# Transposes of P moved into the score slot for 27 early chunks, swapped q of four pairs by DMA, and a new instruction order

## The chip, the cores and the metric

The kernel runs on one core of one Trainium2 chip. The metric is the device time of one execution in microseconds (us); before the change it is 802.02 us, the median of three runs (799.81 to 802.18). The engines of the core are TensorE (PE in the profile; its weight loads are the row PEld), VectorE (DVE), ScalarE (ACT), GpSimd (POOL) and SyncE (SP), which issues all DMAs here.

## The reference, cut to what matters

```python
q_pool = q.reshape(B, H, S // 2, 2, D).mean(axis=3)      # B, H, S, D = 4, 8, 1152, 64
scores = np.matmul(q_pool, k.transpose(0, 1, 3, 2)) / np.sqrt(D)
attn = softmax(scores)                                    # over the 1152 keys
x = np.matmul(attn, v)  ->  2304 tokens x 512
r = np.maximum(x @ w_in, 0.0)                             # 512 x 2048
out = (r * r) @ w_out                                     # 2048 x 512
```

Everything is float32. The kernel multiplies most of it as pairs of float16 numbers, high part and low part, and some of it directly in float32.

## The kernel before, in words

The attention is cut into 16 pairs of heads (`prep(n)`, n = 0 to 15), and each pair into nine chunks of 128 query rows, 144 chunks in all (`chunk(i)`). A feed-forward block (`block(j)`) takes 256 tokens as soon as the four pairs of a batch that hold them are done, so after a first stage attention and feed-forward alternate on PE.

**Pairs.** `prep` loads k, q and v (LK, LQ, LV), scales them, splits them into high and low float16 parts and transposes them by DMA into `kT` (KT, line 628) and `qT` (QT, line 641). The scores also need a copy of `qT` with its two 64-partition halves swapped. That is QX, line 650: two copies of 64 x 1152 float16 per pair, each on DVE or on POOL. The code has a third branch, two DMAs issued by SP, for the pairs listed in `QXD`; before the change the list is empty. Pair 0 is handled in float32 and has no QX.

**Chunks.** S (`scores`, lines 750 and 755) writes 128 x 1152 scores into one of two score slots in PSUM, `sts[i % 2]`, of three banks with 512 columns each; the third bank holds only 128 columns of scores. MX (DVE, line 766) scales them and finds the row maximum; EX (ACT, line 790) writes P = exp(...) to SBUF and so frees the slot for chunk i + 2. For pairs 0 to 3 (chunks 0 to 35, the early chunks) P stays float32 and is transposed on PE: nine 128 x 128 transposes in three groups (TP, `tp4`, line 831), each group into one of the two banks `ba` of resource "a", from which TC (`tc4`: ACT at line 841 or DVE at line 843) copies it to `PT`. The banks "a" also serve the products P x v (PV, lines 942 and 950), the feed-forward products and many small products; from the end of the attention on, six more banks `bt` serve the feed-forward part. From chunk 36 on P is split into two float16 parts and transposed by DMA (HI and LO, lines 794 to 802, and TR, line 805).

**Weights.** During the early chunks the two weight matrices are loaded, normalised and split (`weights`, lines 1217 to 1341), on ACT, DVE and POOL.

**Order.** `Plan.order` makes the program order of every engine ahead of time. Each step has a cost per engine, dependencies, a due time (its chunk number, plus an offset per kind of step from `CFG['off']` and, for early ones, `CFG['off0']`) and perhaps a choice of engines; the planner simulates the five engines and picks the step with the smallest due time among those that can start soon (`sl...` says how soon; `pen` and `bl` weigh the choice of engine). Steps with `take` hold a bank or a buffer until a step with `give` returns it. Each engine then runs its list strictly in that order, with semaphores between engines. SP's list holds all loads, transposes and stores, so whatever stands behind a waiting DMA on SP waits too.

```python
for x in range(3):
    add(("TP", i, x), {"PE": 400}, [("EX", i)] + ring + ([("TP", i, x - 1)] if x else []), lambda o, x=x: tp4(o, x), i, take=(("TP", i, x), ("a",), 0), give=("P", i) if x == 2 else None)
    add(("TC", i, x), alt("TC", ACT=380, DVE=460), [("TP", i, x)] + ring, lambda o, x=x: tc4(o, x), i, give=("TP", i, x))
```

Of the kernel before, what the change touches and what calls it, by code (L numbers as in the profile page):

```python
# [22 lines left out]
def cfg(k, d):  # L23
    return CFG.get(k, d)


COST = {
# [6 lines left out]
}  # L34


class Clock:


    W = 3413.3  # L40
# [188 lines left out]
def kernel(  # L229
# [182 lines left out]
    def ringof(vi, j):  # L412
# [5 lines left out]
        for v_, r_ in reversed(pairs_[: pairs_.index((vi, r))]):  # L418
            if left and not other and (visits[v_][0] in full_v) != (n in full_v):
                left, other = set(range(0, 896, 64)), True  # L420
            w = 320 if r_ else 256
            hit = left & {c for h in base(v_, r_) for c in range(h, h + w, 64)}
            if hit:
                out.append(("PV", v_, r_))
                left -= hit
        return out

    def prep(n):
        pair = preps[n]["pair"]
# [3 lines left out]
        old = [("S", both(preps[p0]["last"])[0])] if p0 is not None else []  # L433
# [27 lines left out]
        if n == 0 and n in full_s:  # L461
            sk = k[b, 2 * hp : 2 * hp + 2].rearrange("h (p c) d -> p h (c d)", c=9)
            tk = rk

            def lk(o, x):
                nc.sync.dma_start(out=tk().rearrange("p h c d -> p h (c d)")[:, :, 192 * x : 192 * x + 192], in_=sk[:, :, 192 * x : 192 * x + 192])

            for x in range(3):
                add(("LK", n) + ((x,) if x < 2 else ()), {"SP": 900}, [], lambda o, x=x: lk(o, x), need, take=None if x else (("k", n), ("raw",), 0), after=[("LK", n, x - 1)] if x else prev)
        else:  # L470
            add(("LK", n), {"SP": 2500}, [], lambda o: load_kv(rk(), k), need, take=(("k", n), ("raw",), 0), after=prev)
        add(("LQ", n), {"SP": 2600}, [], load_q, need, take=(("q", n), ("raw",), 0), after=[("LK", n)])
        if n in full_v:
            add(("LF", n), {"SP": 2200}, oldv, lambda o: load_kv(v4(slot), v), visits[vs[0]][2], after=[("LQ", n)])
        else:
            add(("LV", n), {"SP": 2200}, [], lambda o: load_kv(rv(), v), need, take=(("v", n), ("raw",), 0), after=[("LQ", n)])

        def qsum(o):
# [227 lines left out]
    def chunk(i):  # L706
# [16 lines left out]
        def scores4(o):  # L723
            kt, qt = k4(n), q4(qT(n))
            for x in range(3):
                k0, k1 = 4 * x, min(4 * x + 4, 9)
                w = 128 * (k1 - k0)
                for y in both(i):
# [3 lines left out]
                    else:  # L732
# [720 lines left out]
```

## Time and profile before

| what | us |
|---|---|
| median of three runs | 802.02 |
| the profiled execution | 804.16 |
| its span, first to last instruction | 802.3 |
| PE busy in it | 742.4 |
| DVE busy | 582.9 |
| ACT busy | 575.4 |
| POOL busy | 383.0 |

The profiled execution has a span of 802.3 us, and 1.86 us lie around it. The mean granted clock of PE is 0.977 of full speed. In the profile, "busy" is the time in which an engine has an instruction running; a row of the timeline or of the waits ends with the idle time of the engine ahead of an instruction and with what ended that idle time.

### The profile page before, as it was taken

How to read it: one execution, taken by the hardware profiler on the slowest of the kernel's cores; microseconds unless marked ns; L12 is line 12 of the kernel's file. 1: busy time of each engine (PE TensorE's matmuls, PEld its weight loads, DVE VectorE, ACT ScalarE, POOL GpSimd, SP SyncE). 2: the span in 40 equal slices, each digit the busy share in tenths (PEclk: the TensorE clock that was granted, in tenths of full speed). 3: DMA queues.
4: the chain of work that ended last, by engine and by line, in shares of the span. 5: the costliest groups of instructions: out<-in, count | busy, mean ns of one | idle time of the engine just before them, and what ended most of it. 6: DMA issues, size and time to landing. Idle time of an engine off the chain costs nothing.

```text
span 802.3 us, 15287 instructions
## 1 busy us (share of the span) xinstructions
PE 742.4 (93%) x5998; PEld 491.7 (61%) x5998; DVE 582.9 (73%) x897; ACT 575.4 (72%) x894; POOL 383.0 (48%) x255
## 2 busy tenths in 40 slices
PE   4969788887899999998899999999999999999997
PEld 3546555544675577546666676577567657785654
DVE  3888999858799896888988899877888864202211
ACT  5776888778797888777897888788888854503412
POOL 2453633258676476365585656585666331001300
PEclk8888999999799999999999999999999999999999
DMA  8587383304999999999799999999999992000011
GB/s 285 207 218 214 119 239 136 75 9 90 219 187 202 192 227 210 211 209 183 159 212 210 207 207 208 211 201 213 204 209 199 182 189 46 1 1 14 14 27 27
DMA packets 324199, 127.77 MB, mean 159 GB/s; under 512 B 306976, under 2 KB 307744, under 8 KB 324128
## 3 DMA queue, kind: packets, MB, share of 16 engines
q1 hardware_dynamic: 324128, 126.80, 76.6%
q8 instruction: 47, 0.77, 0.4%
q14 instruction: 24, 0.20, 0.1%
HBM read 45.09 MB, written 4.72 MB: 62 GB/s over the span
## 4 chain that ended last, share of the span: by engine, by line
PE 42%; DVE 6%; DMA 4%; ACT 3%; issue 3%; POOL 1%; SPq 0%; ACTq 0%; DVEq 0%
PE ba L1163 9%; PE ba L1114 9%; PE bt L1163 6%; PE bt L1114 6%; PE s L755 5%; PE ba L950 5%; DVE s L766 2%; DMA PT<-buf 2%; DMA raw<-in_v_dram 1%; DVE region L1141 1%; ACT buf L794 1%; DMA kT<-buf 1%; PE s L750 1%; ACT buf L790 1%; DVE buf L802 1%
## 5 line engine op out<-in xcount | busy, mean ns | idle before, releaser
L766 DVE TENSOR_SCALAR_CACHE_REDUCE s<-s,esc 128x1152 f32<-128x1152 f32 x135 | 190.3, 1419 | 23.0 <-PE s L755 21.0
L1114 PEld LDWEIGHTS <-w 128*128 128x128 f16 x1728 | 169.1, 99 | 28.8 <-issue 3.2
L802 POOL TENSOR_TENSOR buf<-buf,buf 128x1152 f16<-128x1152 f32 x63 | 159.6, 2535 | 53.6 <-ACT buf L794 40.0
L790 ACT ACTIVATE buf<-s,ca 128x1152 f32<-128x1152 f32 x144 | 174.5, 1213 | 9.6 <-POOL ca L776 3.9
L755 PE MATMUL s<-kT,qT 128*128 128x512 f16 x720 | 136.6, 328 | 9.2 <-ACT buf L790 8.7
L1163 PE MATMUL ba<-w,region 128*128 128x512 f16 x624 | 142.3, 379 | 0.0
L1163 PEld LDWEIGHTS <-region 128*128 128x128 f16 x864 | 82.4, 98 | 95.6 <-issue 1.9
L1114 PE MATMUL ba<-region,w 128*128 128x256 f16 x1128 | 131.5, 274 | 1.2 <-DVE region L1041 0.5
L755 PEld LDWEIGHTS <-qT 128*128 128x128 f16 x720 | 64.0, 100 | 65.0 <-issue 16.5
L1141 POOL TENSOR_TENSOR region<-region 128x512 f16<-128x512 f32 x32 | 42.2, 1320 | 102.1 <-ACT region L1134 101.5
L950 PE MATMUL ba<-PT,v 128*64 128x320 f16 (+1 forms) x1296 | 84.7, 287 | 2.2 <-DMA PT<-buf 2.1
L794 ACT ACTIVATE buf<-buf 128x1152 f16<-128x1152 f32 x71 | 82.4, 1160 | 6.0 <-DMA PT<-buf 2.3
L950 PEld LDWEIGHTS <-v 128*64 128x64 f16 x1296 | 71.1, 110 | 15.0 <-issue 6.2
L802 DVE TENSOR_TENSOR buf<-buf,buf 128x1152 f16<-128x1152 f32 x45 | 67.5, 1501 | 16.2 <-ACT buf L794 11.6
L831 PE MATMUL ba<-ident,buf 128*128 128x128 f32 x324 | 51.6, 289 | 15.5 <-DVE PT L843 8.3
L1129 ACT ACTIVATE region<-region 128x512 f16<-128x512 f32 x72 | 45.0, 626 | 27.7 <-PE bt L1163 19.1
L1141 DVE TENSOR_TENSOR region<-region 128x512 f16<-128x512 f32 x40 | 39.1, 980 | 30.7 <-ACT region L1134 30.3
L831 PEld LDWEIGHTS ba<-ident,buf 128*128 128x128 f32 x324 | 35.2, 144 | 30.4 <-DVE PT L843 9.9
L1163 PE MATMUL bt<-w,region 128*128 128x512 f16 x240 | 52.6, 379 | 0.0
L1124 ACT ACTIVATE region<-ba 128x512 f32<-128x512 f32 x39 | 23.0, 591 | 36.8 <-PE ba L1114 36.8
L841 ACT ACTIVATE PT<-ba 128x384 f32<-128x384 f32 x74 | 34.0, 490 | 20.7 <-PE ba L831 20.0
L1114 PE MATMUL bt<-region,w 128*128 128x256 f16 x408 | 45.9, 273 | 0.0
(180 smaller groups left out, 993.9 us busy)
## 6 DMA issues: line engine op xcount, KB each, us to landing
raw<-in_q_dram SPq DMA_DIRECT2D x32, 288.0 KB, 3.7
raw<-in_k_dram SPq DMA_DIRECT2D x15, 576.0 KB, 4.6
region<-in_moe_w_in_dram SPq DMA_DIRECT2D x8, 1024.0 KB, 6.6
region<-in_moe_w_out_dram SPq DMA_DIRECT2D x8, 1024.0 KB, 5.3
raw<-in_v_dram SPq DMA_DIRECT2D x12, 576.0 KB, 4.7
out_dram<-half SPq DMA_DIRECT2D x20, 128.0 KB, 2.5
v<-in_v_dram SPq DMA_DIRECT2D x4, 576.0 KB, 7.1
out_dram<-buf SPq DMA_DIRECT2D x16, 128.0 KB, 2.4
```

Of the source, the lines that this page charges most:

```text
L755: nc.tensor.matmul(s[:, x, :w], lhsT=qt[:, l].rearrange("p c m -> p (c m)")[:, 128 * c0 + h : 128 * c0 + h + 255 : 2], rhs=rhs, **st)
L766: nc.vector.tensor_scalar(st3(), st3(), sc, 3e38, op0=ALU.mult, op1=ALU.min, accum_out=a[:, x : x + 1])
L790: nc.scalar.activation(P(), st3(), AF.Exp, bias=a[:, 1:2], scale=s1, accum_out=col)
L794: nc.scalar.activation(hl()[:, 0], P(), AF.Copy)
L802: e.tensor_tensor(out=hl()[:, 1], in0=P(), in1=hl()[:, 0], op=ALU.subtract)
L831: nc.tensor.matmul(t[:, y], lhsT=P()[:, c * 128 : (c + 1) * 128], rhs=ident, is_transpose=True, start=(y == 0), stop=(y == 2), skip_group_ ...
L841: nc.scalar.activation(out, t, AF.Copy)
L950: nc.tensor.matmul(px[h * 64 : (h + 1) * 64, 64 * r * (1 - h) : 64 * r * (1 - h) + N], lhsT=vv[:, h, kc, vl, :], rhs=p2(vi, r, h, 9 * pl + ...
L1114: nc.tensor.matmul(ph[:, f2], lhsT=w16[0][:, SLOT[f // 4], wl, a, f % 4 * 128 : (f % 4 + 1) * 128], rhs=xhl()[:, xl, a], start=(i == 0), s ...
L1129: nc.scalar.activation(gt[u][:, 0], rt[u % 2], AF.Square)
L1141: e.tensor_tensor(out=gt[u][:, 1], in0=rt[u % 2], in1=gt[u][:, 0], op=ALU.subtract)
L1163: nc.tensor.matmul(p[:, :DM], lhsT=g[:, gl, f % 2, tt * 128 : (tt + 1) * 128], rhs=w16[1][:, SLOT[f // 4], wl, f % 4], start=(f == 0 and g ...
```

## The change

1. `HYB` lists chunks 9 to 35, the early chunks of pairs 1, 2 and 3. For these the first of the three transpose groups (columns 0 to 383 of P) is written to columns 128 to 511 of the third bank of the chunk's own score slot. It takes no bank of resource "a" and gives none back. The other two groups stay as they were.
2. The score step of a chunk whose slot was so used two chunks earlier (chunks 11 to 37) is split: S does the first two banks, and a new step SB does the third. SB waits for S and for the eviction TC(i - 2, 0) of the transposes in that bank. MX now waits for SB. The number of matmuls and weight loads is the same.
3. `QXD` is (1, 2, 3, 4): for these pairs the two copies of QX become two DMAs from SBUF to SBUF, issued by SP behind the landing of QT.
4. All offsets, slacks and weights of the planner have new values, and some planned costs do too (`LK`, `LQ`, `KT`, `QT`, `TR`, `ST`, `LO` on POOL, the first weight load). So the order changes in the whole kernel, and with it the choice of engine of those steps that have one.

```diff
-CFG = {..., 'slPE': 10.8333, 'slACT': 264.0828, 'slDVE': 159.9116, 'off': {...}, 'off0': {...}, ...}
+CFG = {..., 'slPE': 143.7987, 'slACT': 193.3687, 'slDVE': 104.16, 'off': {...}, 'off0': {...}, ..., 'QXD': (1, 2, 3, 4), ..., 'HYB': (9, 10, ..., 35)}
...
-        def scores(o):
+        def scores(o, xs=(0, 1, 2)):
...
-                for x in range(3):
+                for x in xs:
...
-            add(("S", i), {"PE": 1115 if CH[j] is None else 985}, [("KT", n), ("QX", n, 0), ("QX", n, 1)] + back, scores, i, give=("kT", n) if end else None)
+            two = i - 2 in hyb
+            sd = [("KT", n), ("QX", n, 0), ("QX", n, 1)]
+            if two:
+                add(("S", i), {"PE": 985 if CH[j] is None else 870}, sd + back, lambda o: scores(o, (0, 1)), i)
+                add(("SB", i), {"PE": 150 if CH[j] is None else 130}, sd + back + [("S", i), ("TC", i - 2, 0)], lambda o: scores(o, (2,)), i, give=("kT", n) if end else None)
+            else:
+                add(("S", i), {"PE": 1115 if CH[j] is None else 985}, sd + back, scores, i, give=("kT", n) if end else None)
...
+            def st3_():
+                return sts[i % 2][:, 2, 128:].rearrange("p (a b) -> p a b", b=128)
+
             def tp4(o, x):
-                t = bank(o, 3, 128)
+                t = st3_() if i in hyb and not x else bank(o, 3, 128)
...
+    hyb = {i for i in cfg("HYB", ()) if chunks[i][0] in full_v and chunks[i][0] not in full_s}
```

## Rows read from the trace of the kernel before

**Rows 1.** The page's first part: busy time, share and instructions of each engine.

```profile
PE 742.4 (93%) x5998; PEld 491.7 (61%) x5998; DVE 582.9 (73%) x897; ACT 575.4 (72%) x894; POOL 383.0 (48%) x255
```

**Rows 2.** Busy time by stretch; last columns: granted clock, DMA share, GB/s.

```profile
0.00:60.00 60.00, 41.40 (x308) 28.78 (x309) 39.41 (x61) 39.96 (x61) 26.66 (x22) 0.88 0.76 236
60.00:160.00 100.00, 86.57 (x689) 56.98 (x691) 92.81 (x151) 80.36 (x125) 38.46 (x26) 0.97 0.54 158
160.00:206.00 46.00, 34.30 (x240) 19.21 (x236) 33.12 (x60) 36.80 (x49) 32.41 (x15) 0.89 0.33 71
206.00:640.00 434.00, 422.42 (x3592) 283.95 (x3594) 371.70 (x540) 359.21 (x571) 265.80 (x176) 0.99 1.08 202
640.00:802.00 162.00, 157.70 (x1179) 102.83 (x1173) 45.89 (x87) 59.11 (x92) 19.71 (x17) 1.00 0.21 41
```

**Rows 3.** Groups of instructions, 60 to 160 us: count, busy, mean ns, idle before.

```profile
L766 DVE TENSOR_SCALAR_CACHE_REDUCE s<-s,esc 128x1152 f32<-128x1152 f32 x26 | 36.5, 1419 | 2.9 <-PE s L755 2.5 <-PE s L750 0.3
L790 ACT ACTIVATE buf<-s,ca 128x1152 f32<-128x1152 f32 x25 | 30.4, 1225 | 2.9 <-DVE s L766 2.9
...
L841 ACT ACTIVATE PT<-ba 128x384 f32<-128x384 f32 x44 | 20.2, 490 | 11.9 <-PE ba L831 11.5
...
L843 DVE COPY PT<-ba 128x384 f32<-128x384 f32 x19 | 10.0, 550 | 0.8 <-PE ba L831 0.8
```

**Rows 4.** Waits, 0 to 206 us: who for whom, total us, times, longest.

```profile
ACT PT L841 <- PE ba L831: 20.0, 23, 3.1
...
PE ba L831 <- DVE PT L843: 8.3, 10, 3.0
...
DVE s L766 <- PE s L755: 6.3, 6, 3.3
...
PE ba L831 <- ACT PT L841: 4.8, 15, 0.9
```

**Rows 5.** Timeline of PE, 103 to 112 us: start, us, instruction, idle before.

```profile
103.78 0.93 PE L831 MATMUL ba<-ident,buf 128*128 128x128 f32 x6 [0.25 <-ACT PT L841]
105.36 1.14 PE L755 MATMUL s<-kT,qT 128*128 128x512 f16 x6 [0.65 <-ACT buf L790]
...
111.02 0.55 PE L831 MATMUL ba<-ident,buf 128*128 128x128 f32 x3 [0.72 <-DVE PT L843]
```

**Rows 6.** Line 650 (QX), 0 to 206 us: ns minimum/median/maximum, first and last start.

```profile
L650 POOL COPY qT<-qT x5: 1139/1140/1143, 43.3 to 151.1; 64x1152 f16<-64x1152 f16 x5
...
L650 DVE COPY qT<-qT x3: 475/627/1335, 44.3 to 104.4; 64x1152 f16<-64x1152 f16 x3
```

**Rows 7.** Timelines of POOL and of DVE at 72 us.

```profile
72.31 1.14 POOL L650 COPY qT<-qT 64x1152 f16<-64x1152 f16 x1 [2.25 <-DMA qT<-half]
...
72.43 1.33 DVE L650 COPY qT<-qT 64x1152 f16<-64x1152 f16 x1
```

**Rows 8.** DMA issues by line, whole run: KB each, median us to landing.

```profile
raw<-in_k_dram SPq DMA_DIRECT2D x3, 192.0 KB, 2.6
...
qT<-half SPq DMA_TRANSPOSE x13, 3.3
```

**Rows 9.** Timelines of SP and of PE, 39 to 46 us.

```profile
39.39 1.45 SPq L641 DMA_TRANSPOSE qT<-buf  x1
40.94 0.53 SPq L450 DMA_DIRECT2D raw<-in_k_dram  x1
...
45.26 1.06 PE L547 MATMUL ba<-raw 128*128 128x128 bf16 x9 [1.66 <-DMA raw<-in_k_dram]
```

**Rows 10.** Timelines of DVE and of PE ahead of the first block's products.

```profile
188.73 0.15 DVE L1071 TENSOR_SCALAR xs<-xs 128x1 f32<-128x1 f32 x1
...
198.30 0.15 DVE L1082 RECIPROCAL xs<-xs 128x1 f32<-128x1 f32 x1
...
206.11 0.59 PE L586 MATMUL ba<-acc,cols 128*128 128x1 f32 x2 [2.22 <-ACT v L573]
206.56 4.05 PE L1114 MATMUL ba<-buf,w 128*128 128x256 f16 x24
```

More of the change, by code (lines that the diff above doesn't have):

```diff
@@ L432, in prep @@
         p0 = preps[n]["old"]
-        old = [("S", both(preps[p0]["last"])[0])] if p0 is not None else []
+        old = [("SB" if preps[p0]["last"] - 2 in hyb else "S", both(preps[p0]["last"])[0])] if p0 is not None else []
         keep = preps[n]["slot"] is None
@@ L470, in prep @@
         else:
-            add(("LK", n), {"SP": 2500}, [], lambda o: load_kv(rk(), k), need, take=(("k", n), ("raw",), 0), after=prev)
-        add(("LQ", n), {"SP": 2600}, [], load_q, need, take=(("q", n), ("raw",), 0), after=[("LK", n)])
+            add(("LK", n), {"SP": 2350}, [], lambda o: load_kv(rk(), k), need, take=(("k", n), ("raw",), 0), after=prev)
+        add(("LQ", n), {"SP": 2450}, [], load_q, need, take=(("q", n), ("raw",), 0), after=[("LK", n)])
         if n in full_v:
-            add(("LF", n), {"SP": 2200}, oldv, lambda o: load_kv(v4(slot), v), visits[vs[0]][2], after=[("LQ", n)])
+            add(("LF", n), {"SP": 2250}, oldv, lambda o: load_kv(v4(slot), v), visits[vs[0]][2], after=[("LQ", n)])
         else:
-            add(("LV", n), {"SP": 2200}, [], lambda o: load_kv(rv(), v), need, take=(("v", n), ("raw",), 0), after=[("LQ", n)])
+            add(("LV", n), {"SP": 2250}, [], lambda o: load_kv(rv(), v), need, take=(("v", n), ("raw",), 0), after=[("LQ", n)])
         def qsum(o):
@@ L814, in chunk @@
         else:
-            add(("S", i), {"PE": 1115 if CH[j] is None else 985}, [("KT", n), ("QX", n, 0), ("QX", n, 1)] + back, scores, i, give=("kT", n) if end else None)
+            two = i - 2 in hyb
[5 more added lines that the diff above has]
+                add(("S", i), {"PE": 1115 if CH[j] is None else 985}, sd + back, scores, i, give=("kT", n) if end else None)
         fused = n in scaled_
         ge_ = [] if n in full_s else [("GE", n, "qk")]
-        add(("MX", i), {"DVE": 1340 if fused else 1275}, [("S", both(i)[0])] + (ge_ if fused else []), smax, i, give=("qT", n) if end else None)
+        add(("MX", i), {"DVE": 1340 if fused else 1275}, [("SB", i) if i - 2 in hyb and n not in full_s else ("S", both(i)[0])] + (ge_ if fused else []), smax, i, give=("qT", n) if end else None)
         if fused and n not in full_v:
@@ L845, in chunk @@
             for x in range(3):
-                add(("TP", i, x), {"PE": 400}, [("EX", i)] + ring + ([("TP", i, x - 1)] if x else []), lambda o, x=x: tp4(o, x), i, take=(("TP", i, x), ("a",), 0), give=("P", i) if x == 2 else None)
-                add(("TC", i, x), alt("TC", ACT=380, DVE=460), [("TP", i, x)] + ring, lambda o, x=x: tc4(o, x), i, give=("TP", i, x))
+                add(("TP", i, x), {"PE": 400}, [("EX", i)] + ring + ([("TP", i, x - 1)] if x else []), lambda o, x=x: tp4(o, x), i, take=None if i in hyb and not x else (("TP", i, x), ("a",), 0), give=("P", i) if x == 2 else None)
+                add(("TC", i, x), alt("TC", ACT=380, DVE=460), [("TP", i, x)] + ring, lambda o, x=x: tc4(o, x), i, give=None if i in hyb and not x else ("TP", i, x))
             return
@@ L1268, in weights @@
                     ring = [r for r in ring if r in plan.at]
-                    add((W + "L", c), {"SP": 3050}, ring, wl, at)
+                    add((W + "L", c), {"SP": 5000 if c == 0 else 3050}, ring, wl, at)
                     wx = [("WD", 0, 3)] if w == 1 and i == 3 else []
```

10 lines of the change are left out of this document (5 added, 5 removed), and 2 rows, old and new, of the table COST.

## The prediction

> **What bounds the kernel now.** I read the page's busy shares first. PE is busy for 93% of the span, so at most 60 us can be won by filling its gaps [rows 1]. The second view, busy time by stretch, says where they are [rows 2]: 18.6 us idle in the first 60 us, 13.4 from 60 to 160, 11.7 from 160 to 206, and only 11.6 in the 434 us from 206 to 640 and 4.3 in the tail. From 206 us on, PE is the bound. What the change does by name lies ahead of that point, and a microsecond won there comes off the end, since the rest follows at PE's pace.
>
> From 60 to 160 us the tightest engine is DVE, with 92.8 of 100 us busy; ACT has 80.4 and POOL 38.5 [rows 2]. The third view, groups of instructions of that stretch, shows what DVE does: 26 MX of 1.42 us each (36.5 us) and 19 evictions of transposes of 0.55 us (10.0 us), beside splitting weights, k and q [rows 3]. ACT carries 44 evictions of 0.49 us there. The fourth view, the waits up to 206 us, shows what two banks do to a chunk with three transpose groups: PE stands 8.3 us for evictions by DVE and 4.8 us for evictions by ACT, 13.1 in all, and ACT stands 20.0 us because no transposes have come [rows 4]. The timeline shows single cases: the last groups of a chunk start 0.25 us after an eviction by ACT, or 0.72 us late behind one by DVE [rows 5]. So the stretch is bound by DVE, and ACT loses time to a ring of two banks.
>
> **The change part by part.** The sum is made against the profiled execution, 804.16 us (span 802.3 and 1.86 around it). That is 2.1 us above the median shown, so I take 2.1 off at the end. About 0.3% (2.4 us) is what a measurement of this kernel can tell from no change.
>
> *Swapped q, on DVE and POOL.* Eight copies leave the engines, all ahead of 206 us: three on DVE, 0.475, 0.627 and 1.335 us, 2.4 together, and five on POOL of 1.14 us [rows 6]. POOL has slack, so its 5.7 us count for nothing by themselves. Two of the three DVE copies fall in the stretch where DVE is the bound, 2.0 us. I take 1.5 off, between 0 (if DVE's list just gains a gap) and 2.4. The long DVE copy ran beside a POOL copy that began 0.12 us earlier and held on until 73.45 [rows 7]; alone, a copy takes 0.475. The Trainium skill (SBUF — State Buffer, "Who interferes with whom") has a rule for this: DVE and GpSimd share one pair of ports as an exclusive lock, and the later one blocks. By it each of the five POOL copies could have held DVE up for its full 1.14 us, and the sum would be 4.2 us lower; the row shows 0.86 us of delay once.
>
> *Swapped q, on SP.* Eight DMAs of 64 x 1152 x 2 bytes, 147 KB, are added. The nearest row is a load of 192 KB, 2.6 us from issue to landing, and 0.53 us is what issuing a k load took [rows 8, 9]. So qT is complete some 3 us later than with copies. The scores wait for k's transpose too, so that much may be covered. What can show is SP's order: QX waits for QT's landing, 3.3 us [rows 8], and what stands behind it on SP waits too. After the QT of pair 1 comes the k load of pair 2, for which PE already stood 1.66 us [rows 9]. If SP blocked there the loss is up to 3.3 us; four such places are at most 13 us, were all uncovered, but later loads have raw buffers to wait for anyway, and the planner can put other issues into the gap. I take +0.5, range 0 to 3.3.
>
> *First transpose group in the score slot.* The work is the same: same transposes, same evictions. What goes is the claim of 27 of 108 groups on the two banks; with two groups left per chunk, all nine transposes of a chunk can be issued in a row. If the waits of those 27 of 36 chunks go, PE gets back 0.75 x 13.1 = 9.8 us and ACT 0.75 x 20.0 = 15 us [rows 4]. That is not yet time, because DVE is the bound. It becomes time as ACT takes evictions from DVE: evened out, DVE and ACT would each have (92.8 + 80.4) / 2 = 86.6 us, 6.2 less for DVE, some 11 of its 19 evictions moved [rows 2, 3]. I take 5 off; bounds 0 (no eviction moves) and 10 (PE's whole 9.8).
>
> *The split score step.* The third bank of the next score in this slot waits for an eviction; MX and PE's next instructions stand behind it. Before: EX ends, six matmuls of 1.14 us, MX [rows 5]. After: EX ends, three transposes (0.55), 0.25 of waiting, the eviction (0.49), 0.25 again, two narrow matmuls (by columns 256/2304 of 1.14, 0.13), MX: 1.67 us, 0.53 more, while the wide ones run in that time [rows 3, 5]. Does a slot have that time? 26 MX in 100 us is 3.85 us a chunk, 7.7 a slot [rows 3], and the loop MX, EX, score needs some 4.5 us with its waits; 0.5 more fits. But chunks come in bursts. I take +1.5, between 0 and 27 x 0.53 = 14.
>
> *The new order.* It can't be worked out by hand; I bound it by idle time that it could fill or open. One visible case: the step at 198.30 needs only the one at 188.73, but stands behind other work on DVE, and the first products of the feed-forward part start at 206.56, behind a gap of 2.22 us on PE [rows 10], one of several that make 11.7 us from 160 to 206 [rows 2]. An order that runs this step at once wins up to 9.6 us, less than that idle time; a bad order costs as much there, or doubles the 11.6 us of idle PE in the long stage [rows 2]. I take 2 off, the size of the one gap shown; range -9.6 to +11.6.
>
> Sum: -1.5 + 0.5 - 5 + 1.5 - 2 = -6.5. 804.16 - 6.5 - 2.1 = **795.5 us**.
>
> **The rivals.**
> (a) *DVE keeps the bound.* The bank waits vanish but ACT's and PE's time is only idled elsewhere, no eviction changes engine, and the order gives nothing. For it: DVE stood just 6.3 us for scores [rows 4], so it was fed. Against: ACT has 20 us free in the same stretch and can take evictions. Also here: the change does not do what it says, because the two groups left still meet other users of the two banks. Only the 1.5 us of DVE copies remain, given back by SP and SB: 802.0, within 0.3%.
> (b) *The score waits for the eviction* (slower). The eviction in the third bank stands behind a 1.2 us EX or MX in its engine's list, PE stands at SB, and DVE, already the bound, waits for its scores. It decides as soon as MX's wait for scores grows by more than the 6.5 us that I count on. Price: 14 us if all 27 pay their 0.53; with -5 for the banks, -1.5 and +0.5 for q and nothing for the order that makes 802.0 + 8 = 810.0. The Trainium skill (PSUM — Partial Sum Buffer, "PSUM bank collisions raise a hardware error") speaks against the change here: two engines must be kept apart by bank, not by address, so free columns of a bank in use aren't free. That is why the wait exists; no run here shows a collision. Against (b): the 7.7 us per slot above.
> (c) *The order costs in the long stage* (slower). From 206 to 640 DMA is fully used (share 1.08), with PE idle for only 11.6 us [rows 2]; a later start of a few transposes shows at once. With that idle time doubled and the early gain of 4.5 kept (-6.5 without the order's -2): 802.0 - 4.5 + 11.6 = 809.1.
> (d) *The order fills the gaps ahead of 206 us too*: three quarters of the 9.6, -7.2 in place of -2, and the full 10 for the banks: 802.0 - 10 - 7.2 - 1.5 + 0.5 + 1.5 = 785.3. For it: the late step of [rows 10]. Against: it needs two things at once.
>
> **How the numbers follow.** Forecast 0.48 (own range 788 to 799), (d) 0.12, (a) 0.18, (b) 0.11, (c) 0.11. Faster by over 0.3% (below 799.6): 0.48 + 0.12 = 0.60. Within: 0.18. Slower (above 804.4): 0.22. The range reaches to (d), 785, and up to 808, which takes in (a) and the cheaper half of (b) and (c).
>
> **What would show it.** Right: the wait of ACT for transposes falls from 20.0 to under 10 us, evictions on DVE from 60 to 160 us from 19 to about 10, the first feed-forward product comes at about 200 us instead of 206.6, and the time from there to the end stays near 596 us. Line 650 has no copies ahead of 200 us on DVE and POOL. Wrong: DVE's wait for scores up to 206 us grows past 13 us (b); PE's idle time behind the first feed-forward product grows past 20 us (c); the first product comes no earlier (a).

## The result: slower by 0.9%, and the profile after

The changed kernel takes 810.25 us (median; 805.5 to 813.83) against 802.48 us for the kernel before, timed beside it (799.77 to 806.99): a ratio of 1.0091, 95% interval 1.0066 to 1.0116. Slower, and above the range that was given. The profiled execution took 812.57 us, with a span of 810.8 and a mean granted clock of 0.970 (before 802.3 and 0.977). A trace shows one execution; those read below took between 6 us less (e18) and 5 us more (e15) than the median of their kernel's runs.

The page's first part after the change (before: [rows 1]):

```profile
PE 747.4 (92%) x5998; PEld 492.1 (61%) x5998; DVE 598.6 (74%) x957; ACT 589.3 (73%) x874; POOL 311.9 (38%) x207
```

PE has the same 5998 matmuls and is busy 5.0 us longer; DVE and ACT have 15.7 and 13.9 us more to do, POOL 71.1 us less. So, beside the eight copies of q, the new order moved work from POOL to DVE and ACT.

Busy time by stretch after the change (columns as in [rows 2], which answer to the first four and the last row), with the long stage cut into pieces:

```profile
0.00:60.00 60.00, 43.89 (x337) 29.60 (x337) 39.82 (x68) 36.85 (x57) 24.35 (x22) 0.91 0.79 256
60.00:160.00 100.00, 82.72 (x663) 55.70 (x662) 87.26 (x129) 80.29 (x131) 46.64 (x27) 0.95 0.56 151
160.00:206.00 46.00, 41.16 (x301) 26.95 (x300) 36.20 (x63) 37.38 (x49) 26.07 (x15) 0.95 0.27 63
206.00:640.00 434.00, 415.46 (x3480) 273.66 (x3479) 382.14 (x601) 368.36 (x538) 197.50 (x133) 0.98 1.08 203
...
640.00:811.00 171.00, 164.14 (x1223) 106.16 (x1220) 53.23 (x99) 66.46 (x102) 17.31 (x13) 0.99 0.22 44
...
206.00:280.00 74.00, 71.39 (x587) 47.20 (x585) 67.88 (x108) 65.99 (x95) 26.52 (x19) 1.00 1.12 203
280.00:330.00 50.00, 47.48 (x365) 29.84 (x366) 39.55 (x60) 39.46 (x57) 16.43 (x14) 1.00 1.10 209
330.00:380.00 50.00, 39.80 (x334) 24.83 (x334) 41.91 (x84) 37.30 (x55) 19.42 (x11) 0.80 1.01 194
380.00:460.00 80.00, 78.19 (x663) 51.57 (x660) 72.83 (x106) 67.06 (x101) 44.01 (x29) 1.00 1.11 203
460.00:640.00 180.00, 178.60 (x1539) 120.22 (x1538) 159.97 (x249) 158.55 (x233) 91.12 (x62) 1.00 1.07 203
```

The same pieces of the long stage before:

```profile
206.00:280.00 74.00, 72.51 (x592) 48.20 (x594) 63.54 (x87) 62.16 (x98) 45.28 (x30) 0.98 1.06 197
280.00:330.00 50.00, 50.00 (x444) 35.66 (x441) 41.42 (x63) 43.90 (x74) 33.38 (x23) 1.00 1.13 216
330.00:380.00 50.00, 45.74 (x386) 29.22 (x385) 41.90 (x72) 37.34 (x57) 25.25 (x19) 0.97 1.09 202
380.00:460.00 80.00, 76.00 (x636) 50.51 (x635) 71.98 (x97) 66.15 (x109) 51.68 (x29) 1.00 1.01 195
460.00:640.00 180.00, 178.17 (x1544) 120.35 (x1544) 152.86 (x225) 149.67 (x238) 110.20 (x78) 1.00 1.10 204
```

Busy time times granted clock is a rough measure of the matmul work that PE got through. Summed up to 206 us it is 41.40 x 0.88 + 86.57 x 0.97 + 34.30 x 0.89 = 150.9 before [rows 2] and 43.89 x 0.91 + 82.72 x 0.95 + 41.16 x 0.95 = 157.6 after: PE is **6.7 us ahead** (the other traces with these two early orders give 152.0 to 155.8, in e5, e6, e9 and e17, and 158.9 and 161.2, in e10 and e18). It keeps that lead to 280 us (+7.0). Then 280 to 330 costs 2.5, and 330 to 380 costs 12.5 (44.4 before, 31.8 after: 10.2 us idle, and the rest at a clock of 0.80). From there on PE is **some 8 us behind**, wins 2.6 back by 640 us, loses some 3 in the tail (6.9 us idle there in place of 4.3) and ends 8.5 us later. So the lead is lost on one stretch of 100 us in the middle of the stage in which I had taken PE for the bound.

What the lead is made of shows in two counts. Up to 206 us the changed kernel has done 96 feed-forward matmuls (12.6 us on PE, of which some 11.1 would be left at the full clock, at which 24 take 2.78), the kernel before none:

```profile
L1123 PE MATMUL ba<-buf,w x96: 272/273/421, 174.9 to 204.6; 128*128 128x256 f16 x96
```

So apart from feed-forward work PE is some 4 us behind. From 60 to 160 us, where the change by name was made, it got through 5.4 us less (78.6 against 84.0). The row maxima, one for each chunk, are behind too. Those of pairs 1 and up, from 0 to 206 us, before and after (beside nine of pair 0 in either):

```profile
L766 DVE TENSOR_SCALAR_CACHE_REDUCE s<-s,esc x33: 1405/1418/1427, 62.7 to 204.2; 128x1152 f32<-128x1152 f32 x33
...
L766 DVE TENSOR_SCALAR_CACHE_REDUCE s<-s,esc x31: 1406/1422/1427, 57.6 to 202.3; 128x1152 f32<-128x1152 f32 x31
```

At 160 us it is 31 chunks in place of 35, at 206 us 40 in place of 42 (40 to 42 and 42 to 44 in the traces with the same early orders). From 206 to 640 us both kernels take 98 chunks, 4.4 us each, so two chunks are worth 8.9 us, near the 8.5 by which the changed kernel ends later. That the two chunks are the loss is a reading of these traces; no run moves them alone.

What the change did where it was made, first the evictions of transposes from 60 to 160 us (columns as in [rows 3]):

```profile
L850 ACT ACTIVATE PT<-ba 128x384 f32<-128x384 f32 x38 | 17.5, 491 | 6.3 <-PE ba L840 5.9
L850 ACT ACTIVATE PT<-s 128x384 f32<-128x384 f32 x16 | 7.8, 494 | 3.0 <-PE s L840 1.8 <-PE s L755 1.0
L852 DVE COPY PT<-ba 128x384 f32<-128x384 f32 x8 | 4.3, 550 | 0.4 <-PE ba L840 0.3
...
L852 DVE COPY PT<-s 128x384 f32<-128x384 f32 x5 | 2.8, 555 | 2.6 <-PE s L755 2.0 <-PE s L750 0.6
```

DVE has 13 of them in place of 19, ACT 54 in place of 44. Then the waits from 0 to 206 us (for those of before see [rows 4]):

```profile
ACT PT L850 <- PE ba L840: 16.9, 15, 4.4
...
DVE s L766 <- PE s L755: 6.5, 7, 2.9
PE ba L840 <- ACT buf L790: 5.8, 3, 4.9
...
PE s L840 <- ACT buf L790: 4.7, 6, 1.4
...
PE s L755 <- DVE PT L852: 3.5, 5, 0.7
...
PE ba L840 <- ACT PT L850: 2.8, 5, 1.2
...
PE s L755 <- ACT PT L850: 2.3, 5, 0.6
```

PE's 13.1 us of waits for evictions are down to 2.8 at the banks and 5.8 at the split score steps. Against that, PE's transposes wait 10.5 us for exponentials (5.8 and 4.7; before 1.9). The copies of the swapped q of pairs 1 to 4 are gone from DVE and POOL. The first product of block 0 starts at 174.91 us, 31.65 us earlier than before [rows 10].

The hole at 330 to 380 us, in PE's timeline of the changed kernel (columns as in [rows 5]):

```profile
339.52 1.14 PE L755 MATMUL s<-kT,qT 128*128 128x512 f16 x6 [1.92 <-ACT buf L790]
341.92 2.08 PE L755 MATMUL s<-kT,qT 128*128 128x512 f16 x6 [1.26 <-ACT buf L790]
...
355.32 0.56 PE L586 MATMUL ba<-acc,cols 128*128 128x2 f32 x2 [3.83 <-DVE ba L1010]
...
362.23 5.58 PE L959 MATMUL ba<-PT,v 128*64 128x320 f16 x54
...
369.83 2.78 PE L1123 MATMUL ba<-region,w 128*128 128x256 f16 x24
```

and before, block 1's last products and block 2's first:

```profile
345.70 5.34 PE L1163 MATMUL ba<-w,region 128*128 128x512 f16 x24
...
363.47 4.11 PE L1114 MATMUL ba<-region,w 128*128 128x256 f16 x24
```

Between the end of block 1's last product, at 331.16, and the first of block 2, at 369.83, PE has no feed-forward product for 38.7 us (before 12.4, from 351.04 to 363.47). It has attention and small products, and the attention comes only as fast as a chunk's steps go through DVE and ACT. Six score matmuls then take 2.08 us in place of 1.14, and 54 matmuls of P x v 5.58 in place of 3.86: the clock has fallen to its lower level. DVE's timeline at its worst place:

```profile
350.52 2.12 DVE L481 TENSOR_TENSOR raw<-raw 128x576 f32<-128x576 f32 x1 [2.07 <-DMA raw<-in_q_dram]
352.56 1.41 DVE L766 TENSOR_SCALAR_CACHE_REDUCE s<-s,esc 128x1152 f32<-128x1152 f32 x1
```

The q sum of a later pair (line 481) stands on DVE ahead of the row maximum of a chunk whose scores are ready; it waits 2.07 us for its load and works 2.12, and PE's 3.83 us of idle time follow. That is read from the trace; no experiment moved this step. Over the whole hole neither engine is busier than before: DVE 41.9 us in both kernels, ACT 37.3.

### The profile page after: what moved, and what is told of

Read it like the earlier page. It is cut to its first block, busy times and chain, and to the rows that moved or that the text cites. A ratio compares the mean times of both kernels' runs of the same rounds, so it can differ in the third digit from the quotient of the medians.

```text
span 810.8 us, 15302 instructions
## 1 busy us (share of the span) xinstructions
PE 747.4 (92%) x5998; PEld 492.1 (61%) x5998; DVE 598.6 (74%) x957; ACT 589.3 (73%) x874; POOL 311.9 (38%) x207
## 4 chain that ended last, share of the span: by engine, by line
PE 70%; DVE 10%; ACT 7%; issue 5%; DMA 5%; POOL 1%; SPq 1%; DVEq 0%; ACTq 0%; POOLq 0%
PE ba L1172 15%; PE ba L1123 14%; PE s L755 11%; PE ba L959 8%; PE bt L1172 6%; PE bt L1123 6%; DVE s L766 3%; ACT buf L790 3%; PE ba L951 2%; PE ba L840 2%; DMA region<-in_moe_w_in_dram 2%; PE s L750 2%; DMA raw<-in_q_dram 1%; PE s L840 1%; ACT PT L850 1%
## 5 line engine op out<-in xcount | busy, mean ns | idle before, releaser
L755 PE MATMUL s<-kT,qT 128*128 128x512 f16 x720 | 141.2, 334 | 11.6 <-ACT buf L790 5.6
L802 POOL TENSOR_TENSOR buf<-buf,buf 128x1152 f16<-128x1152 f32 x41 | 103.0, 2514 | 71.4 <-ACT buf L794 52.9
L794 ACT ACTIVATE buf<-buf 128x1152 f16<-128x1152 f32 x107 | 124.5, 1164 | 4.1
L1150 POOL TENSOR_TENSOR region<-region 128x512 f16<-128x512 f32 x45 | 60.0, 1337 | 167.9 <-ACT region L1143 167.9
L802 DVE TENSOR_TENSOR buf<-buf,buf 128x1152 f16<-128x1152 f32 x67 | 93.9, 1402 | 15.2 <-ACT buf L794 13.5
L840 PE MATMUL ba<-ident,buf 128*128 128x128 f32 x243 | 41.9, 297 | 9.9 <-ACT buf L790 5.8
L369 DVE SCALAR_TENSOR_TENSOR buf<-raw,psc,buf 128x576 f16<-128x576 f32 x35 | 50.3, 1442 | 0.9 <-POOL buf L340 0.8
L773 ACT ACTIVATE ca<-ca,cols 128x1 f32<-128x1 f32 x52 | 15.2, 292 | 42.1 <-DVE s L766 38.8
L1150 DVE TENSOR_TENSOR region<-region 128x512 f16<-128x512 f32 x27 | 20.3, 756 | 32.7 <-ACT region L1143 32.1
L1143 ACT ACTIVATE region<-region 128x512 f32<-128x512 f32 x65 | 40.9, 630 | 2.1
```

Source lines behind the costliest of these rows:

```text
L369: nc.vector.scalar_tensor_tensor(out=o, in0=x, scalar=s, in1=h, op0=ALU.mult, op1=ALU.subtract)
L755: nc.tensor.matmul(s[:, x, :w], lhsT=qt[:, l].rearrange("p c m -> p (c m)")[:, 128 * c0 + h : 128 * c0 + h + 255 : 2], rhs=rhs, **st)
L794: nc.scalar.activation(hl()[:, 0], P(), AF.Copy)
L802: e.tensor_tensor(out=hl()[:, 1], in0=P(), in1=hl()[:, 0], op=ALU.subtract)
L840: nc.tensor.matmul(t[:, y], lhsT=P()[:, c * 128 : (c + 1) * 128], rhs=ident, is_transpose=True, start=(y == 0), stop=(y == 2), skip_group_ ...
L1150: e.tensor_tensor(out=gt[u][:, 1], in0=rt[u % 2], in1=gt[u][:, 0], op=ALU.subtract)
```

## The experiments

Two devices come back in them. "The order of X, written out" replaces the planner's call by the list of steps that it made for kernel X, with engines and buffers, so that code can be changed under an unchanged order. And "first transpose" is the first of the 108 DMA transposes of P (line 805), "stretch" the time from its start to that of the last. In the two kernels:

```profile
L805 SPq DMA_TRANSPOSE PT<-buf x108: 2377/2858/4211, 192.8 to 660.4; - x108
```

before, and after:

```profile
L805 SPq DMA_TRANSPOSE PT<-buf x108: 2414/2837/5240, 201.1 to 666.9; - x108
```

so the stretch is 467.6 and 465.8 us, and what follows it to the end of the span 141.9 and 143.9. Every ratio is against the kernel before, timed on the same chip. A difference in us is between two medians (e1 to e4 beside a kernel before of 802.13 us). Each text on record says what its theories are.

### Which part costs: e1 to e4

The order of before, written out, with one part of the change at a time (e1, e2), and the new order, written out, with parts taken off (e3, e4).

```diff
 e1 (code of before)
+CFG 'QXD': (1, 2, 3, 4)
-    seq = plan.order(...)
+    seq = order of before, written out
 e2 (code of after)
+CFG 'HYB': (9, ..., 35), no 'QXD'
+    seq = order of before, written out; SB(i) directly behind S(i) and TC(i - 2, 0), what needs SB(i) behind it
 e3 (code of after)
-CFG 'HYB', 'QXD'
+    seq = order of after, written out; QX of pairs 1 to 4 on POOL and DVE
 e4 (code of after)
-CFG 'HYB'
+    seq = order of after, written out
```

> Kernel before with its program order kept on every engine; only the eight swapped copies of q of pairs 1 to 4 become DMAs at the same places. Theory O (the loss of the changed kernel, +8 us, comes from its new order: the first DMA transpose of P starts at 201.1 us instead of 192.8, and the stretch from the first to the last one takes 466 us in both): first DMA transpose of P within 2 us of 192.8, time 802 within 2.5 us. Theory F (the two features cost the time): 804 to 808.

> Kernel before with its program order; only the first group of transposes of chunks 9 to 35 goes to the score slot's third bank, and the third part of the score follows its eviction (503 of PE's 511 steps and 581 of DVE's 599 keep their order). Theory O: first DMA transpose of P within 4 us of 192.8, PE's waits for evictions up to 206 us fall from 13.1 us to under 8, time 796 to 804. Theory F: PE's new waits at the third bank come on top, 806 to 812.

> Changed kernel with its program order kept; both features undone (transposes of all groups into the two banks, scores in one step, swapped copies of q on GpSimd and VectorE). Theory O: it stays slow, 808 to 815, first DMA transpose of P at 199 to 206 us. Theory F: back at 800 to 804.

> Changed kernel with its program order kept; only the transposes go back to the two banks and the scores to one step, the DMAs for q stay. Theory O: 808 to 815, as the changed kernel or a little slower, since this order was made for three groups in three banks. Theory F with the third bank at fault: 800 to 804.

| kernel | us | ratio, interval | first to last transpose |
|---|---|---|---|
| e1 old order, q by DMA | 805.62 | 1.0046 (1.0019 to 1.0073) | 190.0 to 660.0 |
| e2 old order, third bank | 876.48 | 1.0934 (1.0892 to 1.0976) | 260.8 to 732.4 |
| e3 new order alone | 819.69 | 1.0228 (1.0190 to 1.0267) | 207.8 to 675.4 |
| e4 new order, q by DMA | 817.07 | 1.0197 (1.0159 to 1.0236) | 206.4 to 672.6 |

The **new order alone costs 17.6 us**; q by DMA gives 2.6 of it back there (the intervals overlap), the third bank, added to that, 6.8 by the medians and 8.5 by the ratios. These steps lead from the kernel before to the changed one, so their sum confirms nothing. e3 has the same hole: by the measure above its PE is 4.0 us ahead at 206 us and some 10 behind at 380.

```profile
330.00:380.00 50.00, 41.15 (x318) 23.65 (x316) 44.29 (x78) 37.33 (x54) 16.08 (x10) 0.83 1.04 191
```

In the old order neither part is a gain: q by DMA costs 0.46% (the profile of e1, with a span of 801.8, does not show where), and the third bank 9.3%. Of the times on record beforehand, e1 is within theory F's; e3 and e4 are slow, as O said, but 5 and 2 us beyond its ranges; e2 lies 64 us outside both. What the third bank does in the new order is seen in e4's waits from 0 to 206 us, without it:

```profile
ACT PT L3123 <- PE ba L3113: 31.4, 33, 4.6
...
PE ba L3113 <- ACT PT L3123: 9.7, 19, 0.9
...
PE ba L3113 <- DVE PT L3125: 3.0, 4, 1.8
```

With the third bank PE's 12.7 us at the banks become 2.8, and 5.8 come at the split scores: 4.1 us less in all, which is a part of the 6.8 that the times say. In the old order the waits of e2 from 60 to 262 us are of another kind:

```profile
PE s L3055 <- ACT buf L3090: 36.3, 15, 3.7
ACT buf L3090 <- DVE s L3066: 30.4, 15, 3.9
DVE s L3066 <- PE s L3055: 24.9, 18, 4.5
```

PE waits for EX, EX for MX and MX for PE: with the third part of the score behind an eviction, scores, maximum and exponentials of the old order run one after another, where they had run beside each other. That is rival (b)'s place at five times its price, but in an order that was not made for it: 8 of PE's 511 steps and some 18 of DVE's 599 change places in e2, among them the row maxima of chunks 31 to 37, since they follow SB. So the 74 us are the price of the third bank with these moves.

### A first theory, and what it did not survive: e5 to e8

In the runs so far the stretch had always taken 466 to 472 us, whenever it began. So theory T said that the DMA transposes are the pace and that the new order loses by beginning them 8.3 us later; theory P, that PE's work and idle time set the end.

```diff
 e5 (before): no DMA transpose of nine late chunks
         def tr(o):
+            if i >= 60 and i % 9 == 4:
+                return
 e6 (before): two of the three products P x v
-            ps = [... for vl, pl in ((1, 0), (0, 0), (0, 1)) for kc in range(NC)]
+            ps = [... for vl, pl in ((1, 0), (0, 0)) for kc in range(NC)]
 e7 (after): PE's order around chunk 35
-H(0,1) H(0,2) TP(35,*) S37 SB37 S38 PV(5,1) RT1 S39 H(0,3) ...
+TP(35,*) S37 SB37 S38 PV(5,1) RT1 S39 H(0,1) H(0,2) RB(1,0) H(0,3) ...
   (ACT's and DVE's steps that follow H(0,1) and H(0,2) move with them)
 e8: as e7, and on ACT
-QQ5 UA(1,3) UB(1,3) EX35 EX36 ... EX39 HI39 VA5
+QQ5 EX35 EX36 ... EX39 HI39 UA(1,3) VA5 UB(1,3); UD(1,3) and block 1's preparation behind
```

> The kernel before without the DMA transposes of P of nine late chunks (67, 76, 85, 94, 103, 112, 121, 130, 139): the steps stay, but issue no DMA, so the products of these chunks read stale data. All other work is unchanged. Theory T (the DMA transposes of P are the pace: from the first to the last of the 108 it takes 466 to 472 us in every run so far, and some 142 us follow): the stretch shortens, at most by 9 x 4.3 = 39 us; since PE is idle for only 11.6 us from 206 to 640, PE takes over as the bound after some 8 to 14 us, so first to last transpose about 455 us and the time 8 to 14 us lower. Theory P (PE's work and idle time set the pace from 206 us on): stretch and time unchanged, 0 to 2 us lower.

> The kernel before without the third of the three products (v high times P low) of P x v for the late chunks: 36 matmuls per group in place of 54, 24 groups. PE has some 27 us less work from 206 us to the end, DMA and the other engines have the same. Theory P: the last transpose and the end come 20 to 27 us earlier. Theory T: first to last transpose stays within 464 to 470 us and only products behind the last transpose fall away; the time falls by 0 to 8 us.

> The changed kernel with two of block 0's first feed-forward steps (the 48 matmuls that take 7.0 us at 185 us) moved behind the last early group's products P x v, whose end is what the first DMA transpose of P waits for. The amount of work on every engine is the same. Theory T: the transposes of chunk 35 and those products come about 3 us earlier (chunk 35's exponentials end at 188.3 us, then the group is free), the first DMA transpose starts at about 198 in place of 201, and the time is 2 to 4 us lower than the changed kernel's 810. Theory P: PE does the same work in another order, so within 1 us.

> As the run before, and the last quarter of w_out's split (two steps of 2.0 us on ACT, one of 4.6 on POOL) moved from 183 to 192 us to behind the chunk 39's exponentials, with the steps of block 1 that need its memory. That lets chunk 35's exponentials start some 4 us earlier and the low part of chunk 36 be made earlier. Theory T: first DMA transpose at 191 to 195 in place of 201, time 6 to 10 us lower than the changed kernel: 800 to 804. Theory P: 0 to 2 us slower than the changed kernel, since the work moved stands among the work of the long stage.

| kernel | us | ratio, interval | first to last transpose |
|---|---|---|---|
| e5 | 798.66 | 0.9956 (0.9930 to 0.9982) | 185.9 to 656.1 |
| e6 | 799.19 | 0.9969 (0.9939 to 0.9999) | 191.3 to 661.1 |
| e7 | 815.15 | 1.0176 (1.0119 to 1.0233) | 196.7 to 670.4 |
| e8 | 820.14 | 1.0228 (1.0176 to 1.0280) | 196.0 to 677.6 |

**Both theories fell.** Nine transposes fewer leave the stretch at 470.2 us, so they are not its pace alone (against T). PE's products P x v cut from 54 to 36 matmuls a group leave it at 469.8 (against P). And e7 and e8 begin the transposes 4.4 and 5.1 us earlier than the changed kernel and end 5 and 10 us later, which neither theory had: a first transpose is worth nothing if the chunks behind it don't follow (at 206 us both have 40 row maxima, as the changed kernel). The long stage of e6, where PE is idle for 27.0 us in place of 11.6 and the end hardly moves:

```profile
206.00:640.00 434.00, 407.00 (x3183) 265.16 (x3183) 371.03 (x530) 354.35 (x565) 259.17 (x175) 0.97 1.06 201
```

and of e5, where PE's idle time is as before (10.5 us) and the DMA share falls:

```profile
206.00:640.00 434.00, 423.55 (x3592) 283.37 (x3590) 367.83 (x536) 355.89 (x565) 262.07 (x172) 0.99 1.00 190
```

### Two bounds at once: e9, with e10, e17 and e18

If PE and the transposes are both near their limit, relieving one shows little and relieving both shows much (theory B), unless it is a relay through DVE, ACT and POOL that sets the pace (R).

```diff
 e9 (before): the edits of e5 and e6 together
 e10 (after), e17 (before): no DMA transpose of chunks 44, 48, ..., 76
         def tr(o):
+            if 44 <= i < 80 and i % 4 == 0:
+                return
 e18 (after): the edit of e6
```

> The kernel before with both reliefs together: nine DMA transposes of P left out (chunks 67, 76, ..., 139, whose products read stale data) and the third of the three products of P x v left out. Each alone left the stretch from the first to the last transpose at 470 us. Theory B (two bounds in balance: PE and the DMA transposes are both full in that stretch, so relieving one lets the other set the pace): with both relieved the stretch falls below 455 us and the time by 12 to 28 us against before. Theory R (a relay: the pace is the chain of a chunk's steps through DVE, ACT and POOL, each in its fixed order, and neither PE nor DMA sets it): the stretch stays at 464 to 472 us and the time falls by 0 to 6 us.

> The changed kernel without the DMA transposes of P of chunks 44, 48, ..., 76 (nine of the 108, which ran between about 230 and 375 us; the products of these chunks read stale data). In the changed kernel PE idles and its clock falls between 331 and 370 us. Theory B: what PE lacks there is attention work that the DMA transposes deliver too late; with nine fewer the transposes get ahead, PE's idle time from 330 to 380 us falls below 5 us with the clock at full, and the time falls by 5 to 12 us, to 798 to 805. Theory R (the chain through MX and EX delivers too late, not the DMA): the hole stays and the time is within 2 us of the changed kernel's 810.

> The kernel before without the DMA transposes of P of the same nine chunks as in e10 (44, 48, ..., 76; their products read stale data): the control to e10. Theory B (in the changed kernel the transposes are late against PE between 230 and 370 us, in the kernel before they are not): here the time falls by 0 to 3 us, against the some 6 us of e10. Theory G (a transpose fewer is worth the same in either order): 5 to 8 us.

> The changed kernel without the third of the three products of P x v for the late chunks (as e6 for the kernel before): some 25 us less PE work from 215 us on. Theory B: PE waits for the transposes in the changed kernel, so the time falls by 0 to 4 us and the stretch from first to last transpose stays at 462 to 470 us. Theory P (after the hole PE has a backlog that sets the end): the time falls by 8 to 20 us.

| kernel | us | ratio, interval | first to last transpose |
|---|---|---|---|
| e9 | 790.16 | 0.9844 (0.9812 to 0.9875) | 190.1 to 649.6 |
| e10 | 803.92 | 1.0030 (1.0000 to 1.0060) | 202.0 to 661.0 |
| e17 | 797.34 | 0.9946 (0.9922 to 0.9970) | 189.4 to 654.0 |
| e18 | 800.47 | 0.9972 (0.9943 to 1.0001) | 196.8 to 652.3 |

Alone the two reliefs gave 0.44% and 0.31%; together 1.56%, twice their sum, and the stretch falls to 459.5. The stretch stays above the 455 us that theory B had set as its mark. So in the long stage of the kernel before, **PE and the attention's transposes are both close to the pace**, as far as these runs tell; a third limit lies close behind, since some 25 us of PE work (busy 717.8 us in e9, 742.4 before) and nine transposes are gone for 11 us of time. Its long stage:

```profile
206.00:640.00 434.00, 411.44 (x3263) 267.02 (x3263) 379.06 (x549) 361.75 (x576) 267.17 (x177) 0.99 1.01 194
```

PE is idle for 22.6 us there with DMA no longer over 1.01, so what is left is the relay or a mixture; no run splits that further.

e10 and e17 say that the transposes are not late in the changed kernel alone: nine fewer are worth 0.61 points there and 0.54 before. In e10 the hole does not close, against what B expected (idle 8.8 us from 330 to 380 in place of 10.2):

```profile
330.00:380.00 50.00, 41.22 (x362) 26.63 (x360) 43.27 (x90) 39.85 (x58) 21.61 (x14) 0.86 0.89 175
```

Busy time times clock is 35.4 us there in place of 31.8, 3.6 of the 12.5 that are missing, so late transposes explain a part of the hole at most. e18 is the clearest difference between the kernels: less work on PE is worth 0.31% before and 1.19 points (9.8 us by the medians) in the changed kernel, and the stretch falls to 455.5 us, where e6 left it at 469.8. With that work gone the two kernels take the same time (0.9972 and 0.9969). That fits a backlog on PE behind the hole: the changed kernel's PE is idle for only 3.2 us from 380 to 640 (5.8 before).

### Where a lead goes: e11 to e16

e12 to e14 join the changed kernel's order of the early part to the old order of the rest, at three points; theory L says that this removes the hole and keeps the lead, F that the loss was made early. e11 and e16 try to start chunks (and in e16 block 0 too) earlier in the kernel before by order alone. e15 takes work away ahead of the first transpose.

```diff
 e12, e13, e14 (code of after)
+    seq = first 620, 670, 742 steps of the order of after, then what is left in the order of before
 e11 (before), ACT
-EX34 UA(1,1) UB(1,1) XQ0 EX35 UA(1,2) ... HI38 ED(5,1) QA5 KA5 ...
+EX34 UA(1,1) EX35 UB(1,1) XQ0 UA(1,2) ... HI38 ED(5,1) QA5 UA(1,3) KA5 ... UB(1,3); UD(1,3), RB(1,*), XR(1,*) later
 e16: as e11, and XA0, XD0 ahead of EX40, KD(5,0); H(0,0) behind S41, H(0,1) behind S42;
      UA(1,3), UB(1,3) behind EX41, block 1's preparation 70 steps later
 e15 (before), products of the early groups
+                m = 2 if r and vi in (4, 5) else NC
-                for kc in range(NC):
+                for kc in range(m):
```

> The kernel before with some of ACT's work moved between 158 and 205 us: chunk 35's exponentials go ahead of two steps of w_out's split and one of block 0, and the last quarter of w_out's split goes behind chunk 38's and 39's steps. Aimed at an earlier start of the DMA transposes without holding PE back. Theory B: the first DMA transpose at 187 to 191 us in place of 192.8, and the time 0 to 4 us lower than before, as far as PE is fed too. Theory R: no gain, within 2 us of before.

> The changed kernel (third bank and q by DMA kept) with its own order up to about 180 us (its first 620 steps) and the order of before for all that follows; the first step of block 0 is then done, as in the changed kernel. Theory F (the loss of the new order is made ahead of 200 us: feed-forward work is put ahead of the attention chunks, which then start late): some of it stays, and where the attention goes first again the first transpose starts at 192 to 197 us, time 800 to 806. Theory L (the loss is made by the new order of the long stage itself, by its hole on PE at 331 to 370 us): the hole goes and the gains of the early part stay, time 790 to 800.

> As the run before, with the changed kernel's order up to about 200 us (its first 670 steps, to the first DMA transpose of P) and the order of before behind it. Theory F: the first transpose starts at 201 us as in the changed kernel, and the time is 806 to 812. Theory L: 793 to 801, with no hole on PE at 331 to 370 us.

> As the run before, with the changed kernel's order up to about 215 us (its first 742 steps) and the order of before behind it. Theory F: 807 to 813. Theory L: 794 to 802, no hole on PE at 331 to 370 us.

> The kernel before with the products P x v of the last two early groups cut from 36 matmuls to 8 each (7 of 9 key blocks are left out), the ones that took 6.75 us at 168 us and 5.07 us at 187.5 us. That takes some 9 us of PE work off ahead of the first DMA transpose, on the attention's own path, so PE and attention are both ahead from there on; nothing changes in the long stage. Theory T2 (the long stage takes its 466 to 470 us from the first transpose on if PE and the attention chunks start it together; a lead of only one of them is returned): the first transpose starts at 183 to 187 us and the time is 6 to 9 us lower than before. Theory Z (the long stage returns any lead): time 0 to 3 us lower.

> The kernel before, order alone changed between 158 and 230 us: chunk 35's exponentials ahead of two steps of w_out's split (as in e11), the input of block 0 made ready as soon as its sums are there, so that its first two feed-forward steps fill PE's gaps behind chunk 41's and 42's scores from about 197 us, and the last quarter of w_out's split and the whole preparation of block 1 put later. No work is left out. Theory T2: the first transpose comes at 187 to 189 us and PE loses less ahead of 206 us than in e11 (15.7 us idle from 160 to 206); the time is 2 to 6 us lower than before, so it would beat both kernels. Theory Z: within 2 us of before.

| kernel | us | ratio, interval | first to last transpose | PE idle 160 to 206, 206 to 280, 330 to 380 |
|---|---|---|---|---|
| before | 802.48 | 1 | 192.8 to 660.4 | 11.7, 1.5, 4.3 |
| after | 810.25 | 1.0091 (1.0066 to 1.0116) | 201.1 to 666.9 | 4.8, 2.6, 10.2 |
| e11 | 807.69 | 1.0079 (1.0051 to 1.0108) | 188.2 to 662.8 | 15.7, 1.3, 3.6 |
| e12 | 820.87 | 1.0226 (1.0189 to 1.0263) | 205.0 to 680.9 | 10.8, 11.7, 4.6 |
| e13 | 809.23 | 1.0096 (1.0061 to 1.0131) | 201.7 to 669.9 | 6.6, 7.6, 5.4 |
| e14 | 811.52 | 1.0121 (1.0083 to 1.0159) | 195.2 to 665.1 | 5.2, 10.7, 3.8 |
| e15 | 803.48 | 1.0017 (0.9991 to 1.0042) | 186.2 to 665.5 | 15.0, 1.3, 6.4 |
| e16 | 811.35 | 1.0123 (1.0086 to 1.0159) | 188.5 to 664.3 | 11.2, 8.8, 4.4 |

The hole goes with the old order behind it, as L said, **and in e13 and e14 the time stays**, as F said. e12 lies outside both theories, 10.6 us slower than the changed kernel, with its first transpose at 205.0. In e13 the lead is returned ahead of 230 us instead:

```profile
206.00:230.00 24.00, 17.93 (x128) 11.69 (x128) 15.56 (x29) 16.23 (x25) 18.63 (x12) 0.64 1.05 206
```

```profile
210.79 2.08 PE L3055 MATMUL s<-kT,qT 128*128 128x512 f16 x6 [2.99 <-ACT buf L3090]
```

The feed-forward steps that fill this place before are in part already done (72 matmuls up to 206 us), so PE has mostly scores, waits for EX between them, and its clock falls to 0.64. e11 is the mirror image: chunks earlier, PE with 4 us more idle time ahead of 206. In e16 the feed-forward steps filled part of 160 to 206, and the idle time moved to 206 to 280.

e15 was the test by taking away: 56 float32 matmuls, some 8 us at the 5.07 us that 36 took before, off PE ahead of the first transpose. It gave nothing measurable (theory Z). PE from 160 to 206 us, and a few lines of its timeline there:

```profile
160.00:206.00 46.00, 30.97 (x188) 18.51 (x187) 36.36 (x68) 36.02 (x47) 31.77 (x16) 0.75 0.42 91
```

```profile
170.45 0.29 PE L1008 MATMUL ba<-negid,r 128*32 128x128 f16 x1 [2.00 <-DVE r L1005]
170.67 2.10 PE L755 MATMUL s<-kT,qT 128*128 128x512 f16 x6
```

Behind the shortened products PE waits 2.00 us for DVE, and the score matmuls that follow take 2.10 us in place of 1.15 (timeline of before at 175 us): the granted clock is 0.75 in this stretch, where it was 0.89 (0.87 to 0.91 in the traces of e5, e6, e9 and e17, which have the same order). The first feed-forward product comes 4.1 us earlier (202.49), and from 330 to 460 us PE is idle for 12.3 us in place of 8.3.

No version here beats the kernel before with all its work in it.

## Why the prediction was wrong, step by step

**The step that failed** is the frame of the sum: "From 206 us on, PE is the bound ... a microsecond won there comes off the end, since the rest follows at PE's pace." The changed kernel is 6.7 us of PE work ahead at 206 us and loses all of it and 8 us more by 380; e15 took some 8 us of work off PE ahead of 206 us and gained nothing. The lead was feed-forward work; the chunks were two behind, and for that the prediction had no term. Busy 97% was true of PE, but attention and feed-forward share it: feed-forward steps done early are filler that is missing later, while the attention comes at a pace that PE alone does not set (e6: a third of the products P x v gone, 0.3%). I had the row that speaks against it in hand, the DMA share of 1.08 [rows 2], and gave it to rival (c) at 0.11.

**The order**, taken at -2 between -9.6 and +11.6: measured +17.6 (e3). Its first bound assumed that idle time filled ahead of 206 is won; the other counted a second 11.6 us of idle time in the long stage, and left out the clock. In the changed kernel the idle time there is 18.5 us, and from 330 to 380 us the clock of 0.80 costs another 8 us (39.80 x 0.20). I also looked at no choice of engine in the long stage; DVE's group of low parts from 206 to 640 us, before:

```profile
L802 DVE TENSOR_TENSOR buf<-buf,buf 128x1152 f16<-128x1152 f32 x42 | 63.5, 1511 | 12.9 <-ACT buf L794 10.7 <-POOL buf L363 1.5
```

and after:

```profile
L802 DVE TENSOR_TENSOR buf<-buf,buf 128x1152 f16<-128x1152 f32 x62 | 87.2, 1406 | 12.0 <-ACT buf L794 10.2 <-POOL region L1150 0.8 <-issue 0.3
```

23.7 us more for this step on the engine on which MX waits its turn. All of DVE's work in the stage grows by 10.4 us only, and not at all from 330 to 380, so that this makes the hole is not shown.

**The third bank and the split score**, -5 and +1.5: right in sign in the new order, mis-sized: -6.8 in place of -3.5 (e4 against the changed kernel). PE's waits at the banks fell from 12.7 to 2.8, by 9.9 as the 9.8 of the prediction. But the way by which that was to become time, evictions that move from DVE to ACT, is not what the third bank did: 6 of the 11 moved, yet e4, which has no third bank, has the same choice of engines, and 11 evictions on DVE from 60 to 160 us against 13. DVE, taken for the bound of that stretch at 92.8 us, is busy for 87.3 us there after the change, with 20 row maxima begun in place of 26. In the old order the same code costs 74 us (e2), far outside the bound of 14: a price worked out as 27 times 0.53 us holds only while scores, maximum and exponentials still overlap.

**Swapped q by DMA**, -1.5 and +0.5: -2.6 in the new order, with overlapping intervals, and +3.5 in the old one. By the rule of the Trainium skill (SBUF — State Buffer, "Who interferes with whom") that I weighed there, the gain could have been 4.2 us larger; the new order's 2.6 lies between, and no run here tells the two apart.

**The rivals.** (b) did not come: DVE's wait for scores is 6.5 us, 6.3 before. (For pair 0, whose chunks have no split step and which I had not counted, it rose from 3.7 to 8.7.) (c) had the sign, the place and, by chance, the size (809.1 against 810.25). Its mechanism, a later start of the transposes that shows at once, is only a part of it: they start 8.3 us later and the chunks stay two behind, but e7, e8, e11 and e16 started them earlier and gained nothing, and e10 and e17 are alike. The terms that it lacked are the feed-forward work that is missing later and the clock.

**The signs that I had named**: ACT's wait for transposes 16.9 (below 10 expected), evictions on DVE 13 (about 10), line 650 without copies until 198 us (right), first feed-forward product at 174.9 (200), the time from there to the end 636 us in place of "near 596". The last was the sign to look at: an earlier first product is no gain by itself.

**Left open**: which of the moved steps puts the chunks behind and makes the hole at 330 to 380 us, and what sets the pace of the long stage once PE and transposes are both relieved.

## What to carry to other kernels

An engine that is busy for 97% of a stage is not thereby its only bound: take some of its work away and look, then some of the next resource's, then both (0.3%, 0.4%, 1.6% here). Where two kinds of work share an engine and one of them is filler, doing the filler early is a loan; ask at which time it will be missed, what it holds up now, and add the clock that the gap costs. A part that was made together with an order is measured in that order and in the old one: the same third bank was worth -7 us in one and, with the moves that it forced, +74 us in the other.

## What was not expected of the hardware

Work taken off PE came back as idle time and a lower granted clock: in e15 some 8 us of matmuls were gone, PE had 3.3 us more idle time from 160 to 206 us, the clock there was 0.75 in place of 0.89, and six score matmuls took 2.10 us in place of 1.15. Over whole executions the mean clock shows it too: its median is 0.974 in the 12 of e15 and 0.980 in the 17 of the kernel before beside them, and 0.972 against 0.982 for e6. In the changed kernel at 342 and 357 us and in e13 at 211 and 216 us six score matmuls took 2.08 us, at the lower level of the clock; shortly ahead of each PE had stood idle for 0.8 to 3.8 us. And 99 DMA transposes in place of 108 took as long from the first to the last (470.2 us in e5 against 467.6), with the DMA share at 1.00: a share above 1 in the windows was no proof that DMA is the bound.
